# A bank for q's maxima, a three-part subtraction, integer weight assembly and a new step order, in a linear attention followed by two MLPs

## The chip, the cores and the metric

The kernel runs on one core of a Trainium2 chip. The metric is device time in microseconds (us) of one execution, lower is better. TensorE (PE) multiplies matrices, VectorE (DVE) and ScalarE (ACT) do elementwise work, GpSimd (POOL) does a little of it, and SyncE (SP) issues nearly all DMAs.

## The reference, cut to what matters

```python
def phi(x):                                   # q, k: (4, 8, 576, 64)
    proj = einsum('bhsd,df->bhsf', x, w_phi)  # w_phi: (64, 128)
    proj = proj - max(abs(proj), axis=-1, keepdims=True)
    return concatenate([exp(proj), exp(-proj)], axis=-1)
q_p, k_p = phi(q), phi(k)
kv = einsum('bhsf,bhsd->bhfd', k_p, v);  z = sum(k_p, axis=2)
x = einsum('bhsf,bhfd->bhsd', q_p, kv) / (einsum('bhsf,bhf->bhs', q_p, z)[..., None] + 1e-6)
x = x.transpose(0, 2, 1, 3).reshape(2304, 512)
h = ((x @ w1) * (x @ w2)) @ w3                # w1, w2: (512, 1024), w3: (1024, 1024)
x = h @ w_out                                 # (1024, 512)
r = maximum(x @ w_in, 0.0)                    # (512, 2048)
out = (r * r) @ w_out2                        # (2048, 512)
```

The MLP weights arrive as 64-bit floats, which the kernel reads as pairs of 32-bit words and turns into 32-bit floats itself.

## The kernel before

**Attention.** The work is 16 pairs of heads (4 batches, 4 pairs each). A pair has 512 tokens and a tail of 64; the tails of two pairs share tiles. For each pair named steps are run; the order in which the engines get them is written out by hand: `START` for the first slots, then `SLOT` for even and `ODD` for odd slots, then `END`, which lets attention run into the first products of the MLP. In slot t most steps serve pair t; `turn_k`, `turn_q` and their `high`/`low` parts already serve pair t+1, `out`, `keep`, `keep_values`, `reciprocals` and `quotients` serve pair t-1, `turn_x` and `keep_x` pair t-2. Each engine executes its own instructions in the order of the list.

**The steps of q.** `project_q` and `project_qt` multiply q and its tail by w_phi into the PSUM tiles `pq[0]` (two banks) and `pq[1]` (one bank, of which 128 of 512 columns are used). There is one such set, so a pair's projection waits until `exp_q1` and `exp_qt` of the pair before have read it. `max_q` and `max_qt` (DVE, L455) take maxima over blocks of 32, `max_rows` (PE, L463) transposes them into `pm`, `max_parts` (DVE, L468 to L471) takes the rest of the maximum and splits it into a high and a low part, `send` (SP, L477) copies the two by two small DMAs into the tile `mrow`, and `minus_q` (PE, L485) subtracts them from `pq` with three matmuls against a tile of -1. `exp_q0`, `exp_q1` and `exp_qt` (ACT, L492 and L499) follow.

**The other steps.** `project_k`, `peak_k`, `less_k`, `exp_k` do the same for k, whose maximum needs no transposing; `values` multiplies exp(k) by v (L513), `out` multiplies exp(q) by that (L545, L553) into the PSUM tile `po`, `keep` (ACT, L561) copies `po` out, `reciprocals` and `quotients` (DVE, POOL) divide, `turn_x` (PE) transposes the result into `po` again and `keep_x` copies it out. Before the change `pm` is a part of `po`, so `out` has to wait until `max_parts` has read it.

**Weights.** There are 72 blocks of 128x512 weights: 18 are decoded beside attention (the list `beside`; the steps `w-1`, `w0`, `w1` advance them, some seven advances a block and about one block a slot), 54 during the MLPs. `decoding` loads a block (`w-1`), scales the high word on ACT (L149), shifts it and puts the sign in on DVE (L151, L154), isolates the exponent and scales the low word by it on DVE (L158, L161), and adds the two as floats on POOL or, for the second MLP, on DVE (L166). Then the weight is split into a rounded part (ACT) and a rest (POOL or DVE).

Of the kernel before, what the change touches and what calls it, by code (L numbers as in the profile page):

```python
# [31 lines left out]
project_k0/0 low_tail/-1 project_qt/0 max_q/0 max_qt/0 peak_k0/0 fetch_q/0 project_k2/0 less_k0/0 exp_k0/0 max_rows/0  # L32
max_parts/0 project_k1/0 send/0 w-1/0 turn_k/0 high_k/0 peak_k1/0 less_k1/0 warm2/0 w0/0 peak_k2/0 exp_k1/0 less_k2/0
store_x/0 w0/0 low_k/0 warm4/0 turn_q/0 minus_q/0 high_q/0 w0/0 values0/0 values1/0 keep_values/0 exp_q0/0
fetch_tails/0 out/0 project_k1/1 exp_k2/0 keep/0 fetch_q/1 tail_values/0 load_v/0 store_x/1 exp_q1/0 exp_qt/0 low_q/0
project_q/1 keep_values/1 project_qt/1 project_k0/1 w0/0 fetch_k/1 turn_k/1 max_q/1 max_qt/1 w0/1 w-1/1 peak_k0/1 w1/1
max_rows/1 max_parts/1 high_k/1 w1/1 less_k0/1 send/1 low_k/1 peak_k1/1 less_k1/1 exp_k0/1 out/1 turn_q/1 keep/1
exp_k1/1 turn_tails/1 high_q/1 reciprocals/1 quotients/1 minus_q/1 exp_q0/1 w0/1 values0/1 exp_q1/1 exp_qt/1 low_q/1
w0/1 fetch_q/2 keep_tails/1 w0/1 values1/1 low_tail/1 project_k0/2 w0/2 tail_values/1 fetch_k/2 project_q/2
keep_values/2 project_qt/2 turn_x/2 keep_x/2 max_q/2 max_qt/2 project_k1/2 turn_k/2 max_rows/2 peak_k0/2 less_k0/2  # L40
# [17 lines left out]
fetch_k/13 project_q/13 fetch_q/13 project_qt/13 tail_values/12 turn_x/13 w0/13 keep_values/13 keep_x/13 project_k0/13
max_q/13 max_qt/13 turn_k/13 w1/13 w1/13 max_rows/13 peak_k0/13 less_k0/13 max_parts/13 exp_k0/13 send/13 w-1/13
project_k1/13 store_x/13 out/13 high_k/13 keep/13 peak_k1/13 less_k1/13 turn_q/13 low_k/13 turn_tails/13 exp_k1/13  # L60
reciprocals/13 quotients/13 high_q/13 minus_q/13 keep_tails/13 x_load/13 exp_q0/13 values0/13 w0/13 low_tail/13
exp_q1/13 exp_qt/13 w0/13 values1/13 low_q/13 w0/13 load_v/13 tail_values/13 keep_values/14 project_q/14 project_qt/14
turn_x/14 keep_x/14 project_k1/14 max_q/14 max_qt/14 project_k0/14 w1/14 w0/14 peak_k0/14 turn_k/14 less_k0/14
high_k/14 max_rows/14 max_parts/14 send/14 w-1/14 w1/14 exp_k0/14 out/14 peak_k1/14 keep/14 less_k1/14 exp_k1/14
reciprocals/14 quotients/14 low_k/14 turn_q/14 project_k2/14 peak_k2/14 minus_q/14 values0/14 less_k2/14 high_q/14
exp_q0/14 low_q/14 w0/14 w0/14 exp_q1/14 exp_qt/14 values1/14 exp_k2/14 project_q/15 project_qt/15 tail_values/14
turn_x/15 late/15 max_q/15 max_qt/15 w0/14 keep_values/15 keep_x/15 w1/15 w1/15 project_k0/15 peak_k0/15 w0/15
project_k1/15 less_k0/15 max_rows/15 max_parts/15 peak_k1/15 x_split0/15 x_split1/15 exp_k0/15 out/15 send/15
store_x/15 x_split2/15 product_a0/15 keep/15 minus_q/15 reciprocals/15 quotients/15 less_k1/15 w0/15 exp_k1/15
exp_q0/15 w-1/15 values0/15 x_split3/15 values1/15 turn_w3/15 product_a1/15 w0/15 keep_a/15 split_w3/15 w0/15  # L70
tail_values/15 prefetch/15 product_b/16 exp_q1/15 exp_qt/15 keep_values/16 w1/17 turn_w3b/16 turn_x/16 keep_x/16 w1/16
# [1403 lines left out]
```

## Time and profile before

| | |
|---|---|
| runs of this kernel | 918.45, 919.26, 919.79 us; median 919.26 |
| the profiled execution | 918.55 us, of which the span from first to last instruction is 916.8 us |
| PE busy | 886.7 us (97% of the span) |
| DVE, ACT, POOL busy | 646.0, 382.4, 112.5 us |
| granted TensorE clock | 0.999 of full |
| attention | about the first 200 us, the MLPs the rest |

The profile is of one execution. Busy times are sums over the span; a group's mean is the length of one instruction, and the lengths of pipelined instructions overlap, so starts are the better measure of what one costs its engine.

### The profile page before, as it was taken

To read this page: it belongs to the slowest core of one execution; us is meant where nothing else is said; L and a number is where in the kernel's file an instruction comes from. 1 tells how busy PE (TensorE), PEld (TensorE's weight loads), DVE (VectorE), ACT (ScalarE), POOL (GpSimd) and SP (SyncE) were. 2 spreads that over 40 slices of the span, in tenths; PEclk is the share of its full clock that TensorE was granted. 3 is DMA by queue.
4 is the path that set the end of the run, shared out by engine and by line. 5 is a ranking of instruction groups with operands and counts; after the bars stand their busy time and mean duration, and the time that the engine had idled before them with its cause. 6 is when DMAs were issued, how large, how long until landed. Compare 5 with 4: busy or idle time off the path is not lost.

```text
span 916.8 us, 16526 instructions
## 1 busy us (share of the span) xinstructions
PE 886.7 (97%) x6468; PEld 775.1 (85%) x6468; DVE 646.0 (70%) x1215; ACT 382.4 (42%) x733; POOL 112.5 (12%) x112
## 2 busy tenths in 40 slices
PE   8889888899999999999999999999999999999998
PEld 6777777778888888998888889998889898989896
DVE  7877777778987788679999956566754447643533
ACT  5877777763434424454354422222421213321211
POOL 2333333322311450000000000000000000000000
PEclk9999999999999999999999999999999999999999
DMA  7456455547362436557898698597585655684621
GB/s 214 113 139 156 143 137 160 154 117 178 79 179 70 138 93 189 213 195 261 265 355 311 224 393 329 178 305 245 186 287 211 248 223 176 202 332 180 228 94 69
DMA packets 120653, 182.71 MB, mean 199 GB/s; under 512 B 60736, under 2 KB 80000, under 8 KB 120576
## 3 DMA queue, kind: packets, MB, share of 16 engines
q1 hardware_dynamic: 119520, 180.85, 59.9%
q8 instruction: 51, 0.84, 0.4%
q10 hardware_dynamic: 1056, 0.82, 0.3%
q14 instruction: 26, 0.21, 0.1%
HBM read 140.54 MB, written 40.89 MB: 198 GB/s over the span
## 4 chain that ended last, share of the span: by engine, by line
PE 86%; ACT 4%; DVE 4%; DMA 4%; issue 2%; SPq 0%; DVEq 0%
PE op L1321 21%; PE pa L252 11%; PE pb L252 10%; PE yp L1028 10%; PE ph_y L1285 8%; PE ph_x L1285 5%; PE ph_w L1285 5%; PE pf L955 5%; PE po L545 3%; DMA pair<-pair_hbm 2%; PE pq L440 2%; ACT kp L432 1%; PE pk L316 1%; DVE kmax L415 1%; ACT qp L492 1%
## 5 line engine op out<-in xcount | busy, mean ns | idle before, releaser
L1321 PE MATMUL op<-pair,r 128*128 128x512 f32 x864 | 202.9, 390 | 0.0
L1321 PEld LDWEIGHTS op<-pair,r 128*128 128x128 f32 x864 | 161.7, 188 | 32.2
L1028 PE MATMUL yp<-g,w3o 128*128 128x512 f32 (+1 forms) x480 | 105.1, 368 | 0.0
L1028 PEld LDWEIGHTS yp<-g,w3o 128*128 128x128 f32 x480 | 84.2, 189 | 15.0
L252 PE MATMUL pa<-c,w_w12a 128*128 128x512 f32 (+1 forms) x432 | 93.9, 366 | 0.0
L252 PE MATMUL pb<-c,w_w12b 128*128 128x512 f32 (+1 forms) x432 | 93.6, 365 | 0.0
L1285 PE MATMUL ph_y<-yf_t,pair 128*128 128x384 f32 x432 | 87.4, 336 | 0.1
L252 PEld LDWEIGHTS pa<-c,w_w12a 128*128 128x128 f32 x432 | 75.1, 189 | 13.7 <-DVE c L218 0.4
L252 PEld LDWEIGHTS pb<-c,w_w12b 128*128 128x128 f32 x432 | 75.2, 189 | 13.1
L1285 PEld LDWEIGHTS ph_y<-yf_t,pair 128*128 128x128 f32 x432 | 76.0, 188 | 1.5 <-DMA pair<-pair_hbm 0.7
L1372 DVE TENSOR_TENSOR u<-ph_y,m 128x384 f32<-128x384 f32 x24 | 13.4, 558 | 72.1 <-PE ph_y L1285 70.6
L1285 PE MATMUL ph_x<-yf_b,pair 128*128 128x384 f32 x288 | 58.4, 337 | 1.2 <-DMA pair<-pair_hbm 1.2
L1195 ACT ACTIVATE g<-g 128x512 fp32r<-128x512 f32 (+1 forms) x39 | 23.0, 589 | 81.8 <-DVE g L1193 81.8
L1285 PEld LDWEIGHTS ph_x<-yf_b,pair 128*128 128x128 f32 x288 | 51.2, 188 | 3.4 <-DMA pair<-pair_hbm 1.5
L1298 ACT ACTIVATE r<-m 128x384 fp32r<-128x384 f32 x43 | 22.6, 526 | 73.6 <-DVE m L1297 73.6
L432 ACT ACTIVATE kp<-kp 128x512 f32<-128x512 f32 (+1 forms) x80 | 47.2, 590 | 8.1 <-DVE kp L425 6.8
L545 PE MATMUL po<-kv,qp 128*64 128x65 f32 x1024 | 34.7, 223 | 11.9 <-DVE m L470 11.2
L545 PEld LDWEIGHTS po<-kv,qp 128*64 128x64 f32 x1024 | 31.8, 138 | 15.6 <-DVE m L470 14.7
L955 PE MATMUL pf<-w_wo,w3T 128*128 128x512 f32 x192 | 45.0, 390 | 0.0
L1368 ACT COPY m<-ph_x 128x384 f32<-128x384 f32 x24 | 11.5, 481 | 78.8 <-PE ph_x L1285 78.8
L955 PEld LDWEIGHTS pf<-w_wo,w3T 128*128 128x128 f32 x192 | 36.0, 188 | 7.5
L1299 DVE TENSOR_TENSOR r<-m,r 128x384 fp32r<-128x384 f32 x43 | 24.0, 559 | 25.4 <-ACT r L1298 25.4
(183 smaller groups left out, 1519.1 us busy)
## 6 DMA issues: line engine op xcount, KB each, us to landing
pair<-pair_hbm SPq DMA_DIRECT2D x144, 512.0 KB, 7.3
pair_hbm<-w_w SPq DMA_DIRECT2D x32, 512.0 KB, 6.0
raw_w<-in_moe_w_in_dram SPq DMA_DIRECT2D x16, 512.0 KB, 4.4
raw_w<-in_moe_w_out_dram SPq DMA_DIRECT2D x16, 512.0 KB, 4.6
pair_hbm<-v_w SPq DMA_DIRECT2D x16, 512.0 KB, 7.4
raw_w<-in_moe_w_dram SPq DMA_DIRECT2D x56, 128.0 KB, 3.3
x<-x_hbm SPq DMA_DIRECT2D x12, 512.0 KB, 6.3
yi<-y_hbm SPq DMA_DIRECT2D x12, 384.0 KB, 9.5
```

The costliest lines, as they stand in the source:

```text
L252: nc.tensor.matmul(ps[:, 0:n], a, c, start=kk + i == 0, stop=kk == KD - 1 and i == 2)
L432: nc.scalar.activation(z["kp", j][:, :, s, :], z["kp", j][:, :, 1, :], AF.Exp, scale=1.0 - 2.0 * s)
L440: nc.tensor.matmul(at[:, 0:width], wss[h, b, :], src[h, a, 0:width], start=n == 0, stop=n == 2)
L545: nc.tensor.matmul(po_t[half, j, i * E:(i + 1) * E], z["qp"][:, e, 2 * (i // 2) + j, at][:, half], z["kv"][:, e, j, :], start=i + e == 0, ...
L955: nc.tensor.matmul(pf, a, c, start=n == 0, stop=n == len(todo) - 1)
L1028: nc.tensor.matmul(blk.yp[i][:, 0:blk.n], a, d, start=c == blk.c0 and s == 0, stop=c == blk.c1 - 1 and s == 2)
L1195: nc.scalar.activation(g[:, 0, 0:n], g32[:, 0:n], AF.Copy)
L1285: nc.tensor.matmul(ps_, a, c, start=start and n == 0, stop=n == 5, skip_group_check=not start)
L1298: nc.scalar.activation(r[:, 0], h, AF.Copy)
L1299: nc.vector.tensor_tensor(out=r[:, 1], in0=h, in1=r[:, 0].bitcast(F32), op=ALU.subtract)
L1321: nc.tensor.matmul(z.ops[i], a, d, start=z.p + j + s == 0, stop=z.p == NP2 - 1 and j == 1 and s == 2)
L1372: nc.vector.tensor_tensor(out=u2, in0=y, in1=m1, op=ALU.add)
```

## The change

`pm` moves from `po` into the free columns of `pq[1]`. `mrow` shrinks from 128x1536 to 128x512: the maxima of the three 512-column parts lie in three pairs of rows (0 and 1, 32 and 33, 64 and 65), and each of the three matmuls of `minus_q` contracts over its own two rows, in its own 32-row group of the array, instead of over 128 rows that are mostly zero. The memset of `mrow` goes. In `decoding` the two DVE instructions that isolate the exponent and scale the low word give way to one instruction, on POOL for the 18 blocks beside attention and on ACT for the other 54, and the addition becomes one of integers. `START`, `SLOT`, `ODD` and `END` get a new order of the same steps.

```diff
 SLOT = """
-fetch_q fetch_k project_q project_qt turn_x keep_values keep_x project_k0 max_q max_qt project_k1 w1 w1 w0 turn_k
-peak_k0 max_rows high_k less_k0 max_parts send fetch_tails w-1 store_x exp_k0 out peak_k1 less_k1 keep turn_q low_k
-project_k2 exp_k1 reciprocals quotients peak_k2 less_k2 high_q minus_q exp_q0 values0 low_q w0 w0 exp_q1 exp_qt exp_k2
-w0 values1 load_v
+fetch_q w0 turn_x keep_values project_q max_q project_qt fetch_k project_k0 max_qt w1 project_k1 w1 keep_x fetch_tails
+turn_k peak_k0 w-1 store_x high_k less_k0 exp_k0 max_rows out turn_q peak_k1 project_k2 values0 keep max_parts less_k1
+low_k high_q exp_k1 reciprocals send minus_q quotients values1 peak_k2 exp_q0 w0 w0 exp_q1 exp_qt w0 less_k2 low_q
+exp_k2 load_v
 """.split()
 ODD = """
-fetch_q fetch_k project_q project_qt tail_values< turn_x keep_values keep_x project_k0 max_q max_qt project_k1 w1 w1
-w0 turn_k peak_k0 max_rows high_k less_k0 max_parts send w-1 store_x exp_k0 out peak_k1 less_k1 keep turn_q low_k
-turn_tails exp_k1 reciprocals quotients high_q minus_q keep_tails exp_q0 values0 low_q w0 w0 exp_q1 exp_qt w0 values1
-low_tail load_v tail_values
+fetch_q project_k0 project_q project_qt fetch_k tail_values< max_q keep_values turn_x turn_k max_qt peak_k0 keep_x w1
+max_rows less_k0 w1 project_k1 w0 out high_k w-1 peak_k1 turn_q max_parts exp_k0 less_k1 store_x turn_tails keep low_k
+exp_k1 high_q reciprocals values0 send keep_tails minus_q w0 quotients exp_q0 tail_values w0 exp_q1 values1 low_q
+low_tail exp_qt load_v w0
 """.split()
...
+    beside_attention = [True]
...
-        e, w = y, t.bitcast(F32)
+        w = t.bitcast(F32)
         nc.scalar.activation(y.bitcast(F32), hi.bitcast(F32), AF.Copy, scale=2.0 ** -112)
         yield
-        nc.vector.tensor_scalar(
-            out=t, in0=y, scalar1=4, scalar2=1, op0=ALU.logical_shift_left, op1=ALU.logical_shift_right
-        )
+        nc.vector.tensor_scalar(out=t, in0=y, scalar1=3, scalar2=None, op0=ALU.logical_shift_left)
         nc.vector.scalar_tensor_tensor(
             out=t, in0=hi, scalar=-(1 << 31), in1=t, op0=ALU.bitwise_and, op1=ALU.bitwise_or
         )
         yield
-        nc.vector.tensor_scalar(
-            out=e, in0=t, scalar1=-(1 << 23), scalar2=None, op0=ALU.bitwise_and
-        )
-        nc.vector.scalar_tensor_tensor(
-            out=e.bitcast(F32), in0=lo.bitcast(mybir.dt.uint32), scalar=2.0 ** -52, in1=e.bitcast(F32),
-            op0=ALU.mult, op1=ALU.mult,
-        )
+        if beside_attention[0]:
+            nc.gpsimd.tensor_scalar(
+                out=y, in0=lo.bitcast(mybir.dt.uint32), scalar1=2.0 ** -29, scalar2=None, op0=ALU.mult
+            )
+        else:
+            nc.scalar.activation(y, lo.bitcast(mybir.dt.uint32), AF.Copy, scale=2.0 ** -29)
         yield
-        (nc.vector if name.startswith("w2") else nc.gpsimd).tensor_tensor(
-            out=w, in0=t.bitcast(F32), in1=e.bitcast(F32), op=ALU.add
-        )
+        (nc.vector if name.startswith("w2") else nc.gpsimd).tensor_tensor(out=t, in0=t, in1=y, op=ALU.add)
...
-        mrow = att.tile([P, NM * 32], F32R, bufs=1, name="mrow")
+        mrow = att.tile([P, 512], F32R, bufs=1, name="mrow")
...
-            z["pm"] = po_t[:, 0, 3 * P:4 * P]
-            nc.tensor.transpose(z["pm"], z["m1"], ident)
+            z["pm"] = pq[1][:, P:2 * P]
+            nc.tensor.matmul(
+                z["pm"], z["m1"], ident, is_transpose=True, start=False, stop=True, skip_group_check=True
+            )
...
-                    mrow[s:s + 1].bitcast(F32).rearrange("s (k r) -> s k r", r=32), z["mh"][:, s].bitcast(F32)
+                    mrow[s:s + 65:32].bitcast(F32).rearrange("i (k r) -> i k r", r=32), z["mh"][:, s].bitcast(F32)
...
-            for i, at, n in ((0, 0, C * P), (0, C * P, C * P), (1, 0, 2 * TAIL)):
-                row = i * 2 * C * P + at
+            for i, at in enumerate((pq[0][:, 0:C * P], pq[0][:, C * P:], pq[1][:, 0:2 * TAIL])):
+                two = slice(32 * i, 32 * i + 2)
                 nc.tensor.matmul(
-                    pq[i][:, at:at + n], minus, z["mrow"][:, row:row + n], start=False, stop=True, skip_group_check=True
+                    at, minus[two], z["mrow"][two, 0:at.shape[-1]], start=False, stop=True, skip_group_check=True
                 )
...
-        nc.vector.memset(mrow.bitcast(F32), 0.0)
...
+    beside_attention[0] = False
```

`START` and `END` are rearranged in the same manner (the first even slots and the last slots of attention with them).

## Rows read from the trace of the kernel before

**Rows 1.** Busy time of each engine in two stretches, one in attention, one in the MLPs
```profile
core 0: us, PE busy (x) PEld busy (x) DVE busy (x) ACT busy (x) POOL busy (x), PEclk, DMA share, GB/s
...
100.00:125.00 25.00, 22.26 (x381) 19.82 (x382) 19.23 (x39) 18.25 (x36) 8.68 (x9) 1.00 0.49 142
...
400.00:500.00 100.00, 100.00 (x465) 83.36 (x464) 93.81 (x186) 47.32 (x88) 0.00 (x0) 1.00 0.82 286
```
**Rows 2.** Waits of PE in the first 200 us: total, times, longest
```profile
PE po L545 <- DVE m L470: 11.2, 15, 1.3
PE pq L440 <- ACT qp L492: 6.1, 10, 0.8
```
**Rows 3.** Timeline of PE, slots 8 and 9: start, length, instruction, wait ahead
```profile
98.76 0.97 PE L440 MATMUL pq<-qT,wss 64*128 64x512 f32 x6 [0.69 <-ACT qp L492]
...
100.71 1.67 PE L316 MATMUL pk<-wbd,kT 128*128 128x256 f32 x12
...
102.65 0.27 PE L463 MATMUL po<-ident,m 128*128 128x128 f32 x1
103.56 1.15 PE L545 MATMUL po<-kv,qp 128*64 128x65 f32 x32 [0.64 <-DVE m L470]
...
107.36 0.76 PE L485 MATMUL pq<-mrow,minus 128*128 128x512 f32 x3 [0.30 <-DMA mrow<-mh]
108.04 2.09 PE L513 MATMUL pkv<-vs,kp 128*64 128x65 f32 x64
110.42 0.97 PE L440 MATMUL pq<-qT,wss 64*128 64x512 f32 x6 [0.29 <-ACT qp L492]
...
122.13 0.97 PE L440 MATMUL pq<-qT,wss 64*128 64x512 f32 x6 [0.69 <-ACT qp L492]
```
**Rows 4.** Timeline of DVE, slot 8
```profile
98.50 0.43 DVE L158 TENSOR_SCALAR dy_wo<-dt_wo 128x512 int32<-128x512 int32 x1
98.96 0.69 DVE L161 SCALAR_TENSOR_TENSOR dy_wo<-raw_wo,dy_wo 128x512 f32<-128x512 uint32 x1
...
99.91 1.44 DVE L455 TRANSPOSE_TENSOR_REDUCE m<-pq 128x32 f32<-128x1024 f32 x2
101.70 0.69 DVE L415 TENSOR_REDUCE kmax<-pk 128x4 f32<-128x512 f32 x1 [0.36 <-PE pk L316]
...
103.03 0.27 DVE L468 TENSOR_REDUCE mh<-po 48x32 fp32r<-48x128 f32 x1
...
103.54 0.18 DVE L471 TENSOR_TENSOR mh<-m,mh 48x32 fp32r<-48x32 f32 x1
```
**Rows 5.** Timeline of ACT, slot 8
```profile
106.16 0.70 ACT L561 COPY nd<-po 128x650 f32<-128x650 f32 x1 [1.53 <-PE po L553]
...
107.96 0.58 ACT L357 ACTIVATE qT<-pqt 128x512 fp32r<-128x512 f32 x1
108.44 1.93 ACT L492 ACTIVATE qp<-pq 128x1024 f32<-128x1024 f32 x2
```
**Rows 6.** The two DMAs of send in slots 8 and 9, issue to landing
```profile
L477 SPq DMA_DIRECT2D mrow<-mh x2: 557/564/572, 103.3 to 104.0; - x2
...
DMA to landing us min/median/max: 1.8/2.5/3.2
...
L477 SPq DMA_DIRECT2D mrow<-mh x2: 557/565/573, 115.3 to 116.0; - x2
...
DMA to landing us min/median/max: 1.8/1.8/1.8
```
**Rows 7.** Groups by shape in 30 to 185 us: total busy, mean ns of one
```profile
L166 POOL TENSOR_TENSOR dt_wo<-dt_wo,dy_wo 128x512 f32<-128x512 f32 x7 | 8.9, 1273 | 16.3 <-DVE dy_wo L161 16.3
...
L149 ACT ACTIVATE dy_wo<-raw_wo 128x512 f32<-128x512 f32 x5 | 3.4, 683 | 0.0
```
**Rows 8.** Timelines of POOL and DVE, the same moment in the MLPs
```profile
219.47 1.40 POOL L166 TENSOR_TENSOR dt_w<-dt_w,dy_w 128x512 f32<-128x512 f32 x1 [6.53 <-DVE dy_w L161]
...
219.76 1.66 DVE L161 SCALAR_TENSOR_TENSOR dy_w12a<-raw_w12a,dy_w12a 128x512 f32<-128x512 uint32 x1
```
**Rows 9.** The page's part on DMA queues: packets, MB, share of 16 engines' span
```profile
q1 hardware_dynamic: 119520, 180.85, 59.9%
```

More of the change, by code (lines that the diff above doesn't have):

```diff
@@ L31 @@
 warm6/0 fetch_k/0 turn_q/-1 turn_k/-1 high_q/-1 low_q/-1 high_k/-1 project_q/0 turn_tails/-1 keep_tails/-1 low_k/-1
[L32 to L40, printed above, removed]
@@ L41 @@
-w1/2 high_k/2 max_parts/2 out/2 exp_k0/2 peak_k1/2 fetch_tails/2 send/2 keep/2 load_v/1 less_k1/2 w1/2 turn_q/2 w0/2
-project_k2/2 low_k/2 reciprocals/2 quotients/2 peak_k2/2 exp_k1/2 less_k2/2 minus_q/2 high_q/2 values0/2 store_x/2
-exp_q0/2 exp_q1/2 exp_qt/2 w0/2 w-1/2 w0/2 values1/2 low_q/2 load_v/2 exp_k2/2
+project_k0/0 low_tail/-1 project_qt/0 max_qt/0 max_q/0 peak_k0/0 project_k2/0 less_k0/0 exp_k0/0 project_k1/0
+max_rows/0 max_parts/0 send/0 w-1/0 turn_k/0 fetch_q/0 high_k/0 peak_k1/0 store_x/0 less_k1/0 warm2/0 w0/0 peak_k2/0
@@ new lines @@
+exp_k1/0 less_k2/0 w0/0 low_k/0 warm4/0 turn_q/0 minus_q/0 high_q/0 fetch_q/1 w0/0 values0/0 values1/0 fetch_tails/0
+exp_k2/0 keep/0 keep_values/0 out/0 tail_values/0 exp_q0/0 project_k1/1 load_v/0 store_x/1 exp_q1/0 exp_qt/0 low_q/0
+project_q/1 keep_values/1 project_qt/1 fetch_k/1 project_k0/1 w0/0 w0/1 turn_k/1 max_q/1 high_k/1 max_qt/1 peak_k0/1
+w1/1 w-1/1 max_rows/1 max_parts/1 w1/1 less_k0/1 send/1 peak_k1/1 low_k/1 exp_k0/1 out/1 less_k1/1 turn_q/1 keep/1
+exp_k1/1 turn_tails/1 reciprocals/1 high_q/1 quotients/1 minus_q/1 exp_q0/1 w0/1 values0/1 exp_q1/1 exp_qt/1
@@ new lines @@
+keep_tails/1 low_q/1 w0/1 w0/1 values1/1 low_tail/1 tail_values/1 project_k0/2 fetch_q/2 w0/2 fetch_k/2 keep_values/2
+project_q/2 project_qt/2 turn_x/2 keep_x/2 max_q/2 max_qt/2 project_k1/2 max_rows/2 peak_k0/2 less_k0/2 turn_k/2
+max_parts/2 high_k/2 out/2 w1/2 exp_k0/2 peak_k1/2 keep/2 fetch_tails/2 send/2 load_v/1 less_k1/2 low_k/2 w1/2
+turn_q/2 w0/2 project_k2/2 reciprocals/2 exp_k1/2 quotients/2 peak_k2/2 less_k2/2 minus_q/2 high_q/2 values0/2
+exp_q0/2 store_x/2 exp_q1/2 exp_qt/2 low_q/2 w0/2 values1/2 w-1/2 w0/2 load_v/2 exp_k2/2
@@ L56 @@
+low_tail exp_qt load_v w0
 """.split()
 END = """
[L58 to L71, printed above, removed]
@@ L72 @@
-early/16 split_w3b/16 w0/17 w0/16 out/16 w0/16 gate/16 keep/16 w-1/16 prefetch/17 reciprocals/16 quotients/16 last/16
-w1/17 w1/16 w0/16 w0/17 w0/17 w0/16 w0/17 prefetch/16
+fetch_q/13 fetch_k/13 project_q/13 project_qt/13 turn_x/13 tail_values/12 w1/13 project_k0/13 w0/13 keep_values/13
+keep_x/13 max_q/13 max_qt/13 turn_k/13 max_rows/13 peak_k0/13 less_k0/13 w1/13 max_parts/13 exp_k0/13 send/13
+project_k1/13 store_x/13 out/13 w-1/13 high_k/13 keep/13 peak_k1/13 less_k1/13 turn_q/13 low_k/13 exp_k1/13
@@ new lines @@
+turn_tails/13 high_q/13 reciprocals/13 quotients/13 minus_q/13 keep_tails/13 x_load/13 exp_q0/13 values0/13 w0/13
+low_tail/13 exp_q1/13 exp_qt/13 w0/13 values1/13 low_q/13 w0/13 load_v/13 tail_values/13 project_k0/14 project_q/14
+keep_values/14 project_qt/14 turn_x/14 keep_x/14 project_k1/14 max_q/14 max_qt/14 w1/14 peak_k0/14 less_k0/14
+turn_k/14 high_k/14 w0/14 max_rows/14 max_parts/14 send/14 peak_k1/14 w-1/14 w1/14 out/14 exp_k0/14 keep/14 less_k1/14
+exp_k1/14 reciprocals/14 quotients/14 turn_q/14 low_k/14 project_k2/14 peak_k2/14 minus_q/14 values0/14 high_q/14
@@ new lines @@
+exp_q0/14 low_q/14 exp_q1/14 w0/14 less_k2/14 w0/14 exp_qt/14 values1/14 exp_k2/14 turn_x/15 project_q/15
+project_qt/15 tail_values/14 late/15 max_q/15 max_qt/15 w0/14 keep_x/15 w1/15 w1/15 project_k0/15 peak_k0/15 w0/15
+keep_values/15 project_k1/15 max_rows/15 less_k0/15 store_x/15 max_parts/15 peak_k1/15 x_split0/15 x_split1/15
+exp_k0/15 out/15 x_split2/15 send/15 product_a0/15 keep/15 minus_q/15 reciprocals/15 quotients/15 less_k1/15 w0/15
+exp_k1/15 exp_q0/15 values0/15 values1/15 x_split3/15 turn_w3/15 w0/15 product_a1/15 w-1/15 keep_a/15 exp_qt/15
@@ L74 @@
+split_w3/15 w0/15 tail_values/15 prefetch/15 w0/17 product_b/16 keep_values/16 w1/17 exp_q1/15 turn_x/16 turn_w3b/16
+keep_x/16 w1/16 early/16 out/16 w0/16 gate/16 keep/16 reciprocals/16 prefetch/17 split_w3b/16 w-1/16 quotients/16
+w0/16 last/16 w1/17 w1/16 w0/16 w0/17 w0/17 w0/16 w0/17 prefetch/16
 """.split()
@@ L157, in decoding @@
         yield
-        nc.vector.tensor_scalar(
-            out=e, in0=t, scalar1=-(1 << 23), scalar2=None, op0=ALU.bitwise_and
-        )
-        nc.vector.scalar_tensor_tensor(
-            out=e.bitcast(F32), in0=lo.bitcast(mybir.dt.uint32), scalar=2.0 ** -52, in1=e.bitcast(F32),
-            op0=ALU.mult, op1=ALU.mult,
-        )
+        if beside_attention[0]:
[4 more added lines that the diff above has]
+            nc.scalar.activation(y, lo.bitcast(mybir.dt.uint32), AF.Copy, scale=2.0 ** -29)
         yield
-        (nc.vector if name.startswith("w2") else nc.gpsimd).tensor_tensor(
-            out=w, in0=t.bitcast(F32), in1=e.bitcast(F32), op=ALU.add
-        )
+        (nc.vector if name.startswith("w2") else nc.gpsimd).tensor_tensor(out=t, in0=t, in1=y, op=ALU.add)
         got.append(w)
-        spare[name] = e.bitcast(F32)
+        spare[name] = y.bitcast(F32)
     def decode_splitting(src, name, got, tile_of=unit):
```

## The prediction

> **What bounds the kernel now.** I read the busy times by stretch first, then PE's waits, then the timelines of two neighbouring slots on every engine. The stretches split the kernel: in the MLPs PE is busy for all of its 100 us, in attention for 22.26 of 25 us [rows 1]. So nothing that DVE, ACT or POOL gain in the MLPs can shorten them, and what the change can win lies in the first 200 us. There PE's largest waits are 11.2 us in 15 pieces, `out` waiting for `max_parts` over the shared bank, and 6.1 us in 10 pieces, `project_q` waiting for the exponentials [rows 2].
>
> Summing PE's waits would be the wrong reading, because the slots are a loop. `pq` exists once, so projection follows projection: 98.76, 110.42, 122.13 [rows 3], or 11.66 and 11.71 us a slot. Follow the loop in slot 8. `project_q` starts at 98.76; the maxima run on DVE from 99.91 for 1.44 us; PE is at `max_rows` only at 102.65, behind the k projections; `max_parts` runs on DVE from 103.03 to 103.72 [rows 3, 4]. The second DMA is issued at 104.0 and needs 3.2 us [rows 6], so `minus_q` starts at 107.36, after a wait of 0.30 us for it [rows 3]. ACT is still at qT until 108.44, then does the two exponentials in 1.93 us [rows 5], and the next projection starts. So `out`'s wait of 0.64 us is not a link of this loop by itself: it delays `keep` on ACT (106.16), which stands in front of the exponentials, and in a slot where the DMA lands late that costs nothing. In slot 9 the DMAs land in 1.8 us [rows 6]; there the ACT side is the later one. Six of the 16 slots (0, 2, 4, 6, 8, 10) show a landing above 3.0 us, as slot 8; the other ten read like slot 9.
>
> **The change part by part.** Times in the next two paragraphs are counted from the start of `project_q`, with start-to-start costs from [rows 3 to 5]: projection and its tail 1.17 us, two k projections 1.50, `turn_k` 0.44, k's maximum and its subtraction 0.65 to 0.7 each, `out`, `turn_q` and the third k projection together 3.5 (103.56 to 107.06), half of `values` 1.0, `max_parts` 0.69.
>
> *Even slot, new order.* `turn_x` now stands ahead of `project_q`, under the exponentials' tail, so PE reaches `max_rows` at 3.1 instead of 3.89. But DVE does `peak_k0`, `less_k0` and `peak_k1` first, so `max_parts` runs from 4.6 to 5.3 instead of 4.27 to 4.96. The second DMA goes out at 5.55 and lands at 7.35 (with 1.8 us) or 8.75 (3.2). PE does `out` from 3.4 with no wait, and `values0` before `minus_q`, and is free at 7.9. `minus_q` thus starts at 7.9 or 8.8. ACT, whose `keep` now starts at about 5.95 instead of 7.40, is through `high_q` and `exp_k1` at 8.3. `minus_q`'s length is bounded between the present 0.76 us and 0.49: side by side the three matmuls take one stream of 512 columns instead of 1152, and six matmuls in two 64-row groups already take only 0.97 us [rows 3], so I take 0.49. The exponentials end at 10.35 or 11.25: that is the slot, against 11.66.
>
> *Odd slot.* `project_k0` goes ahead of `project_q`, and `max_parts` again ends near 5.3. ACT has one step more before the exponentials and is ready at 8.45, so the slot takes 10.35 with a landing of 1.8 us and 11.15 with one of 3.2, against 11.71.
>
> A pair of slots falls from 23.37 to 20.7 or 22.4 us: 1.3 or 0.5 us a slot. With the ten short and six long landings of the present trace, 1.0 us a slot; over the 14 slots from the second projection to the last, 14.0 us.
>
> *DVE's two instructions* per weight block, 0.43 and 0.69 us [rows 4], 1.12 us in all, leave DVE between `low_q` and `max_q`. They end just as the projection does, so they cost the loop little now and I count no gain of their own; without them DVE is merely early. In the MLPs their going wins nothing, since PE covers it.
>
> *POOL's new instruction* in attention is not in the trace. Below it is bounded by nothing, above by the two-input form at 1.27 us [rows 7]; I take 1.27. POOL is busy for 8.68 of 25 us [rows 1], and the block that it finishes is needed by ACT about 2.5 us into the next slot, so it is hidden up to a length of some 2.5 us. A POOL instruction can hold a DVE one with two SBUF inputs: such a one took 1.66 us beside a POOL instruction, and 0.69 elsewhere [rows 4, 8]. In the loop only L471 is of that kind, 0.18 us long; the new order puts POOL's work either after the slot's `quotients` or some 2 us ahead of L471. I count nothing, at most 0.97 us a slot.
>
> *ACT's new instruction*, 54 times in the MLPs, is priced by the scaling of the high word, 0.68 us [rows 7]; 37 us in all on an engine that is busy for 47 of 100 us [rows 1]. I count nothing: PE has two or more products of 12 matmuls between what ACT copies out and where it is used. If that cover were gone, it would cost up to 0.68 us a block.
>
> *Queues.* `w-1`, `store_x` and, in slots 2, 6 and 10, the four DMAs of `fetch_tails` now stand in front of `send` on SP. A DMA costs SP about 0.6 us to issue (two in 1.2, [rows 6]). Only the tails reach `send`: four issues and a weight load put it back by some 0.6 us in three slots, 1.8 us. The memset of `mrow` lies under the arrival of the first inputs: nothing. `START` and `END` I leave at nothing, within 3 us either way.
>
> *The shape of the two DMAs.* The destination goes from 48 pieces on one partition to 16 pieces on each of three. The mean packet occupies an engine for 0.599 x 16 x 916.8 / 119520 = 0.073 us [rows 9]. If the 48 pieces went through three engines, 16 packets each, the transfer would take 16 x 0.073 = 1.2 us where three packets take 0.2: up to 1.0 us more, which hits the odd slots for about 0.4 us (the even ones wait for PE), some 3 us in all. I count nothing in the likeliest case and keep 3 for the range. The Trainium skill speaks for the longer one: DMA: Bandwidth & Descriptors, section on why a DMA increments its semaphore by 16, has a copy spread over the largest number of engines up to 16 that divides the slowest dimension of both sides, here 3 and 48 where it was 48 and 48. By that rule the time would be some 3 us above my forecast; no row shows on how many engines a copy runs.
>
> The sum: 918.55 - 14.0 + 1.8 = 906.35 in the measure of the profiled execution (1.75 us of it outside the span). It lies 0.7 us under the median of the three runs, so 907 us to be compared with 919.26.
>
> **The rivals.**
> 1. *PE becomes the bound.* If landing and ACT are quicker than I laid them out, a slot is PE's own work: 22.26/25 of 11.69 us is 10.4 [rows 1, 3], less 0.27 for `minus_q`, 10.1. That saves 1.55 x 14 = 22 us: 897. For it speaks that the new order gives PE something to do at each place where it waited; against it, `max_parts` is later on DVE than it was.
> 2. *The landing decides everywhere.* All landings at 3.2 us, or three engines for each of the two DMAs besides: 0.5 us a slot at best, 7 us less the 1.8 and up to 3, so 912 to 917. For it: the weight load now precedes `send`, and the large loads and stores share the engines with it.
> 3. *Slower: ACT stalls the MLPs.* The new ACT instruction waits for DVE to have read the tile that it overwrites, and the copy of a product out of PSUM stands behind it. With 0.68 us for each of 54 blocks on PE's path, 37 us come on top: up to 944. It decides from 0.23 us a block (12.2/54). Against it: PE is full in these stretches [rows 1], with DVE near full beside it, and DVE loses 1.12 us a block.
> 4. *No change.* The loop is held by ACT's in-order steps at the present pace, and the gain is spent on the tails and on rival 3 in small: 918 to 920.
>
> **How the numbers follow.** My forecast, 902 to 912, gets 0.55; PE's own bound 0.16; landings everywhere 0.14; no change 0.07; slower 0.08. The likeliest time is 907. Leaving out the far end of the first rival and the last two, the range is 897 to 917. What a measurement of this kernel can tell from no change is about 0.2%, or 1.8 us: faster 0.85, same 0.07, slower 0.08.
>
> **What would show it.** In the profile after, PE's wait on `max_parts` at `out` must be gone; successive projections should lie 10.3 to 11.2 us apart, and the interval should follow the landing of the second DMA; `minus_q`'s three matmuls should take about 0.5 us; the MLPs should still show PE at 100% and be as long as before, from the end of attention on. I am wrong if projections lie 11.5 us apart or more, if PE has new waits on ACT after 200 us, or if POOL's new instruction takes above 2.5 us and ACT waits for it in attention.

## The result, and the profile after

The changed kernel takes 905.84 us (median of four runs, 905.21 to 906.49) against 919.52 (four runs too, one more than in the table above): a ratio of 0.985 (95% interval 0.9835 to 0.9869), 13.7 us faster. The forecast was 907. Of the two profiled executions the spans are 916.8 and 904.4 us, 12.4 us apart; the forecast's sum was 12.2.

Where the 12.4 us came from, by the starts of four things in both traces:

| stretch | before | after | gained |
|---|---|---|---|
| up to the second projection | 18.88 | 18.33 | 0.55 |
| second projection to the last (14 slots) | 162.19 | 154.04 | 8.15 |
| last projection to the first product of w_out with w3 (L955, now L953) | 21.05 | 19.42 | 1.63 |
| the rest, to the end | 714.6 | 712.6 | 2.0 |

The loop of slots, from which I had expected 12.2, gave 8.15; the ends and the MLPs, which I had left at nothing, gave the other 4.2. So the total came out right partly by luck: two misses cancel, and the experiments had to say why.

PE's waits of the first 200 us come first, as in [rows 2]: total, times, longest.

```profile
PE pq L483 <- DMA mrow<-mh: 7.0, 9, 2.6
PE pk L312 <- DVE kp L421: 1.7, 4, 0.5
...
PE pq L436 <- ACT qp L490: 1.0, 1, 1.0
```

`out`'s wait for `max_parts` (11.2 us) is gone, and the wait of `project_q` for the exponentials has shrunk from 6.1 to 1.0. In their place PE waits for the copied maxima, once for 2.6 us. The timeline of PE, slots 8 and 9, answers [rows 3]:

```profile
95.42 0.97 PE L436 MATMUL pq<-qT,wss 64*128 64x512 f32 x6
...
98.74 1.15 PE L543 MATMUL po<-kv,qp 128*64 128x65 f32 x32
...
103.25 0.50 PE L483 MATMUL pq<-mrow,minus 2*128 2x512 f32 x3
...
105.33 0.92 PE L312 MATMUL pk<-wbd,kT 128*128 128x256 f32 x6 [0.49 <-DVE kp L421]
106.18 0.96 PE L436 MATMUL pq<-qT,wss 64*128 64x512 f32 x6
...
115.58 0.50 PE L483 MATMUL pq<-mrow,minus 2*128 2x512 f32 x3 [1.68 <-DMA mrow<-mh]
...
118.12 0.96 PE L436 MATMUL pq<-qT,wss 64*128 64x512 f32 x6
```

Slot 8 lasts 10.76 us; `minus_q` starts 7.83 us into it (forecast 7.9), waits for nothing, and its three matmuls take 0.50 us (0.49). Slot 9 lasts 11.94, because `minus_q` waits 1.68 us. All 14 intervals between projections: 10.03, 10.28, **14.41**, 10.77, 10.41, 10.77, 10.42, 10.76, **11.94**, 10.78, 10.76, 10.38, **11.83**, 10.50 (before: 10.39 to 12.01, most of them 11.65 to 11.70). The DMA queue of SP shows what slots 3 and 9 have in common (start, issue time; slot 5, without a wait, stands between them for comparison):

```profile
41.65 0.41 SPq L143 DMA_DIRECT2D raw_wo<-in_moe_w_out_dram  x1
42.16 0.38 SPq L608 DMA_DIRECT2D x_hbm<-xm  x1
43.37 1.94 SPq L475 DMA_DIRECT2D mrow<-mh  x2
...
64.37 0.41 SPq L143 DMA_DIRECT2D raw_wo<-in_moe_w_out_dram  x1
67.00 0.34 SPq L608 DMA_DIRECT2D x_hbm<-xm  x1
68.55 1.64 SPq L475 DMA_DIRECT2D mrow<-mh  x2
...
108.38 0.42 SPq L143 DMA_DIRECT2D raw_w12a<-in_moe_w_dram  x1
109.36 0.34 SPq L608 DMA_DIRECT2D x_hbm<-xm  x1
110.91 1.65 SPq L475 DMA_DIRECT2D mrow<-mh  x2
```

In both, a weight load and a store, 512 KB each, go out just ahead of the two small copies. The same pair stands ahead of them in slots 5, 7 and 11 too, but there the load went out 3.3 to 4.2 us before the first copy, against 1.7 and 2.5 us in slots 3 and 9, and the wait is nothing or, in slot 11, 0.49 us. In slots 6 and 10 a weight load (behind the tails' small ones) goes out 0.8 and 0.65 us before it, without a store, and the wait is at most 0.19 us. Slot 13 has neither ahead of its copies and waits 0.54 us; what makes it 11.83 us long no run here asks. In slot 3 the wait costs more than its 2.63 us. The busy times by stretch show it: in 46 to 49 us PE has next to nothing to do, then the granted clock (the third number from the right) falls:

```profile
46.00:49.00 3.00, 0.36 (x15) 0.23 (x11) 1.94 (x4) 1.17 (x3) 2.92 (x3) 1.00 0.72 246
49.00:52.00 3.00, 3.00 (x41) 2.67 (x43) 0.00 (x0) 2.38 (x5) 1.38 (x2) 0.54 0.00 0
52.00:56.00 4.00, 4.00 (x36) 3.51 (x33) 1.86 (x3) 1.81 (x4) 1.27 (x1) 0.92 0.45 128
60.00:100.00 40.00, 38.73 (x691) 33.96 (x691) 31.29 (x62) 33.41 (x67) 23.51 (x20) 1.00 0.58 168
...
400.00:500.00 100.00, 100.00 (x448) 83.05 (x447) 78.46 (x155) 58.01 (x107) 0.00 (x0) 1.00 0.78 279
```

The mean of 0.54 in 49 to 52 us means that nearly all of that stretch ran at the lower of the two levels, 1.2 of 2.4 GHz. In slots without such a wait PE is now busy for 38.73 of 40 us; before it was 22.26 of 25 [rows 1]. In the MLPs PE is full as before, DVE has fallen from 93.81 to 78.46 us in 100 and ACT risen from 47.32 to 58.01.

The new instructions beside attention (30 to 185 us: total busy, mean ns), to be set against [rows 7]:

```profile
L158 POOL TENSOR_SCALAR dy_wo<-raw_wo 128x512 int32<-128x512 uint32 x6 | 9.8, 1641 | 0.5
L164 POOL TENSOR_TENSOR dt_wo<-dt_wo,dy_wo 128x512 int32<-128x512 int32 x6 | 7.7, 1278 | 0.5
...
L153 DVE SCALAR_TENSOR_TENSOR dt_wo<-raw_wo,dt_wo 128x512 int32<-128x512 int32 x6 | 5.8, 970 | 0.2
L158 POOL TENSOR_SCALAR dy_w12a<-raw_w12a 128x512 int32<-128x512 uint32 x3 | 5.5, 1848 | 0.3
...
L152 DVE TENSOR_SCALAR dt_wo<-dy_wo 128x512 int32<-128x512 int32 x6 | 3.5, 576 | 0.0
```

POOL's instruction is longer than the 1.27 us that I took. DVE's two remaining instructions have stretched: the same two took 418 and 692 ns before, so a block costs DVE 1.55 us where four instructions took 2.23, and the 1.12 us that went give 0.7 net. The new instruction is not the reason; the new order is, which puts POOL's `quotients` (L578) beside them. First slot 8 of this kernel, then slot 8 of the run old_order below, which has POOL's new instruction but the order of before:

```profile
102.72 1.58 POOL L578 TENSOR_TENSOR xd<-nd,rc 128x320 f32<-128x320 f32 x2 [3.80 <-DVE rc L569]
102.92 0.80 DVE L152 TENSOR_SCALAR dt_w12a<-dy_w12a 128x512 int32<-128x512 int32 x1
103.75 1.09 DVE L153 SCALAR_TENSOR_TENSOR dt_w12a<-raw_w12a,dt_w12a 128x512 int32<-128x512 int32 x1
```

```profile
101.93 0.42 DVE L152 TENSOR_SCALAR dt_w12a<-dy_w12a 128x512 int32<-128x512 int32 x1
102.38 0.69 DVE L153 SCALAR_TENSOR_TENSOR dt_w12a<-raw_w12a,dt_w12a 128x512 int32<-128x512 int32 x1
102.44 2.02 POOL L158 TENSOR_SCALAR dy_w12a<-raw_w12a 128x512 int32<-128x512 uint32 x1 [0.75 <-DVE dt_w12a L152]
```

In old_order the means of the first group are 418 and 692 ns again, and in old_decode and behind_lo_act, which have the new order and no such POOL instruction in attention, they are 575 to 577 and 969 to 970.

And the part on DMA queues, against [rows 9]:

```profile
q1 hardware_dynamic: 119104, 180.84, 60.0%
```

There are 416 packets fewer, 13 for each of the 32 copies; each run with the new copy has 119104 packets and each with the old copy 119520. That is what 3 engines in place of 16 make if each of them adds one packet to a copy; no view shows the single engines. The Trainium skill (DMA: Bandwidth & Descriptors, the section on why a DMA increments its semaphore by 16) has 3 engines here, each ending its share with a write to the semaphore, and the count agrees.

### The profile page after: what moved, and what is told of

Its sections match the earlier page's. It is cut to its first block, busy times and chain, and to the rows that moved or that the text cites. A ratio compares the mean times of both kernels' runs of the same rounds, so it can differ in the third digit from the quotient of the medians.

```text
span 904.4 us, 16486 instructions
## 1 busy us (share of the span) xinstructions
PE 886.6 (98%) x6468; PEld 773.7 (86%) x6468; DVE 568.5 (63%) x1070; ACT 412.2 (46%) x787; POOL 147.8 (16%) x130
## 3 DMA queue, kind: packets, MB, share of 16 engines
q1 hardware_dynamic: 119104, 180.84, 60.0%
## 4 chain that ended last, share of the span: by engine, by line
PE 89%; DVE 4%; ACT 3%; DMA 2%; issue 1%; POOL 0%; SPq 0%; DVEq 0%; POOLq 0%
PE op L1319 22%; PE pa L248 11%; PE pb L248 11%; PE yp L1026 11%; PE ph_y L1283 8%; PE ph_x L1283 6%; PE ph_w L1283 6%; PE pf L953 5%; PE pk L312 2%; PE pq L436 2%; DMA mrow<-mh 2%; PE po L543 2%; PE pkv L511 2%; PE pkv L521 1%; PE po L584 1%
## 5 line engine op out<-in xcount | busy, mean ns | idle before, releaser
L1191 DVE TENSOR_TENSOR g<-pb,a 128x512 f32<-128x512 f32 (+1 forms) x39 | 24.8, 636 | 51.9 <-PE pb L248 51.7
L1366 ACT COPY m<-ph_x 128x384 f32<-128x384 f32 x24 | 11.5, 480 | 74.2 <-PE ph_x L1283 74.2
L953 PE MATMUL pf<-w_wo,w3T 128*128 128x512 f32 x192 | 44.9, 390 | 0.0
L451 DVE TRANSPOSE_TENSOR_REDUCE m<-pq 128x4 f32<-128x128 f32 (+1 forms) x32 | 23.2, 762 | 33.9 <-PE pq L436 25.2
L953 PEld LDWEIGHTS pf<-w_wo,w3T 128*128 128x128 f32 x192 | 36.0, 188 | 7.5
```

Of the source, the lines that this page charges most:

```text
L451: nc.vector.tensor_reduce(z["m1"][:, at // 32:(at + n) // 32], pq[i][:, 0:n].rearrange("p (n r) -> p n r", r=32), AX.X, ALU.max, apply_abs ...
L953: nc.tensor.matmul(pf, a, c, start=n == 0, stop=n == len(todo) - 1)
L1191: nc.vector.tensor_tensor(out=g32[:, 0:n], in0=pb[:, 0:n], in1=a_sb[:, 0:n], op=ALU.mult)
```

## The experiments

**Theory.** The slot loop around the single `pq` gains about 1.0 us; two slots lose much of it because large transfers stand ahead of `send`; bank, order and subtraction give the loop's gain together, decoding nothing. **Rivals.** PE's waits simply add up (the bank alone gives most); the copy is late because it runs on three engines; decoding on DVE matters. Each run also has the time of the kernel before on the same chip, 917.8 to 918.1.

### First round: one part alone, or one part undone

**bank_alone**: the kernel before, with `pm` in the free columns of `pq[1]` and nothing else.

```diff
-            z["pm"] = po_t[:, 0, 3 * P:4 * P]
-            nc.tensor.transpose(z["pm"], z["m1"], ident)
+            z["pm"] = pq[1][:, P:2 * P]
+            nc.tensor.matmul(z["pm"], z["m1"], ident, is_transpose=True, start=False, stop=True, skip_group_check=True)
```

> The kernel before with one edit: the transposed maxima go to the free columns of q's second PSUM tile, everything else as before. Loop theory: out's wait of 0.64 us is a link of the loop only in the ten slots where the copies of the maxima land in 1.8 us, so 3 to 6 us are won, 913 to 916 us. Rival, PE's waits add up: the 11.2 us go, about 908. Rival, DVE's relief made the gain: nothing, 918 to 920.

Measured 909.91 us, ratio 0.9902 (0.9885 to 0.9919): 8.0 us from three lines, more than the loop as I had followed it allowed. From slot 3 on the intervals are 10.90 to 11.36 instead of about 11.7. The rival, that the waits add up, was nearer with its 908: `out`'s wait was a link of the loop in nearly every slot, by way of `keep` and ACT's order. ACT's timeline of slot 8, whose projection starts at 98.05, shows it beside [rows 5]:

```profile
104.73 0.70 ACT L563 COPY nd<-po 128x650 f32<-128x650 f32 x1 [0.82 <-PE po L555]
...
107.01 1.93 ACT L494 ACTIVATE qp<-pq 128x1024 f32<-128x1024 f32 x2
```

Counted from the projection, `keep` starts at 6.68 us (7.40 before) and the exponentials at 8.96 (9.68 before): both 0.7 us earlier, as the slot is shorter.

**old_order**: the changed kernel with the four lists `START`, `SLOT`, `ODD` and `END` of before.

> The changed kernel with the four step lists of the kernel before; bank, subtraction and weight decoding as changed. Loop theory: the three edits alone win 4 to 7 us of the 13.7, 912 to 915 us, the rest is the order's. Rivals (waits add up, or DVE's relief): as the changed kernel, 905 to 908.

Measured 902.80, ratio 0.9829 (0.9814 to 0.9843): 3 us *faster* than the changed kernel (2 us by the ratios), outside what either side expected. The new order, as it stands, is a part that costs; the intervals of the two ratios overlap a little, but old_decode_mlp below, with the changed kernel's attention, lies clear of this run (0.9847 to 0.988). PE's waits of this run, first 200 us:

```profile
PE pq L436 <- ACT qp L490: 5.7, 11, 0.9
PE pq L483 <- DMA mrow<-mh: 5.6, 10, 0.8
```

In the old order, with everything else new, ACT holds `project_q` as before, but no wait for the copy exceeds 0.8 us, and from slot 3 to slot 12 the intervals alternate between 11.0 and 10.6 without an exception.

**old_decode**: the changed kernel with the decoding of before, in attention and MLPs.

> The changed kernel with the old weight decoding everywhere (two DVE instructions more a block, no POOL or ACT instruction more). Loop theory: DVE's two instructions now stand in front of the low part of the next q and cost up to 0.5 us in even slots, 906 to 910 us, and the MLPs stay as long. Rival, DVE's relief made the gain: 913 or more.

Measured 914.20 (ten runs, 909.9 to 917.9), ratio 0.9961 (0.9941 to 0.998): 8.4 us lost where I had counted nothing. The runs go with the granted clock: 909.90 us at a mean of 0.998, 917.93 at 0.988. The chain that ended last, in slot 8 of this run (start, length, what):

```profile
104.42 0.88 DVE dt_w12a L152
105.32 1.10 DVE dt_w12a L155
...
106.52 0.44 DVE dy_w12a L159
106.98 0.69 DVE dy_w12a L162
107.67 0.34 DVE kp L426
...
108.15 1.62 PE pk L317 x6
```

All four instructions of a block stand between k's maximum and its subtraction on DVE, and PE waits behind them with the k projection that the new order put ahead of `project_q` (four such waits, 7.0 us in all).

**old_minus**: the changed kernel with `mrow`, `send` and `minus_q` of before (one partition a row, contraction over 128 rows).

> The changed kernel with the old layout of the maxima's rows: one partition per part as destination of the two copies, three matmuls over 128 rows. If the copies land late because they run on three engines instead of 16, PE's wait for them falls from 7.0 us to under 3 and that pays for 0.27 us more in each subtraction: 903 to 907 us. Rival, the landing does not depend on the shape and the loads issued just ahead of the copies delay them: the waits stay, and the longer subtraction costs 2 to 4 us, 908 to 910.

Measured 915.83 (ten runs), ratio 0.9976 (0.9965 to 0.9987): 10 us lost, more than any theory had. PE's wait for the copy rose to 12.1 us, the longest 3.6; in slot 3 the two copies, on sixteen engines, took 5.4 and 5.8 us from issue to landing. Its runs, too, go with the granted clock (914.4 us at 0.998, 918.3 at 0.994). Three engines are not what makes the copy late.

### Second round: the loads behind send, and the subtraction by itself

**behind**: in `SLOT` and `ODD` the loads and the store are issued directly after `send`.

```diff
-... w1 keep_x fetch_tails turn_k peak_k0 w-1 store_x high_k ... reciprocals send minus_q ...
+... w1 keep_x turn_k peak_k0 high_k ... reciprocals send fetch_tails w-1 store_x minus_q ...
-... high_k w-1 peak_k1 ... less_k1 store_x turn_tails ... values0 send keep_tails ...
+... high_k peak_k1 ... less_k1 turn_tails ... values0 send w-1 store_x keep_tails ...
```

> The changed kernel with the weight load, the store of x and the tails' loads issued directly behind send instead of ahead of it, in the even and the odd slots. Theory: it is the two 512 KB transfers ahead of send that make the copy of the maxima land late. In the changed kernel the two slots with both of them ahead of send last 14.41 and 11.94 us, the undisturbed ones 10.4 and 10.77. Then PE's waits of 2.63 and 1.68 us at minus_q go, the slots become 10.4 to 10.8 throughout, and the kernel takes 905.8 - 3.6 - 1.2 = 901 us, 899.5 to 902.5. Rival, the copy is late because it runs on three engines: the transfers stay in the same rings and only change places, waits of 1.5 us or more remain in some slots, 904 to 907.

Measured 902.13, ratio 0.9826 (0.9811 to 0.984). The two long slots are gone: slots 3 and 9 last 10.41 and 10.42 us (slot 13 stays long, 12.16), and the granted clock stays at 1.00 in 30 to 60 us, where it was 0.94. From the second projection to the last it takes 148.88 us, 13.3 less than before; the forecast had 14.0 ahead of its deduction for queues. PE's busy time in the middle slots, same columns as above:

```profile
60.00:100.00 40.00, 39.12 (x699) 34.38 (x697) 30.56 (x63) 32.34 (x66) 20.97 (x19) 1.00 0.58 158
```

Against old_order the new order, with its loads behind, gains 0.7 us, and the intervals overlap: a gain from the order in the whole kernel is not shown. The traces show one in `END`: from the last projection to the first product of w_out with w3 every kernel with the new order takes 19.4 us, every one with the old order and the new bank 20.4.

**behind_oldminus**: behind, with the old subtraction and copy.

> The kernel of the run behind (loads and store directly behind send), with the maxima sent to one partition a row and subtracted by matmuls that contract over 128 rows, as before. Theory: minus_q's start-to-end grows by 0.26 us a slot and the copy of the maxima to one partition lands no later than to three: 14 slots by 0.26, some 4 us more than the run behind, 904 to 907. Rival A, sixteen engines in place of three: the copy lands 1 us sooner where it is awaited, and the time is within 2 us of the run behind. Rival B, the old layout has a cost of its own beside these (it took 915.8 us with the loads ahead of send, 10 us above the changed kernel): 910 or more, with waits above 2 us at minus_q.

Measured 904.86, ratio 0.9858 (0.9843 to 0.9872); its runs (904.28 to 905.79) lie all above those of behind (900.90 to 902.97). The size is near the theory's, its reason is not: the middle slots last 10.48 to 10.88 us, nearly as in behind (10.41 to 11.02) but for one of 11.52. From the second projection to the last 2.9 us are lost, about half of them in slot 1 (11.42 against 10.05, with a wait of 1.30 us for the copy).

**bank_minus**: the kernel before, with the bank and the three-part subtraction; old decoding, old order.

> The kernel before, with the maxima's bank and the three two-row matmuls (and their copy to three partitions), but the old decoding and the old order. Theory: with the bank alone it is 909.9 us and its slots are 10.94 to 10.99; minus_q is 0.26 us shorter, which the loop through the exponentials gives back in each slot: 14 by 0.26 = 3.6 us, so 906.3, 905 to 908; the decoding is then worth the remaining 3 to 4 us to the 902.8 of the old order with everything else new. Rival, DVE's two instructions cost nothing in the old order: 902 to 904, and the three-row subtraction gives 7 us. Rival 2, a copy on three engines lands 1 us later: 909 to 914.

Measured 906.58, ratio 0.9872 (0.9857 to 0.9886). Again the expected sum, and again not from its source: the middle slots are 10.94 to 11.00 us, as with the bank alone. The difference lies in the first two, 12.37 and 10.29 us against 14.07 and 13.43. Matmul or copy? The third round asks. Against old_order, the decoding is worth 3.8 us in the old order (2.0 between the two profiled executions).

**old_decode_mlp**: the changed kernel with the old decoding in the MLPs only.

> The changed kernel with the old decoding in the MLPs' 54 blocks only; attention as changed. Theory: PE is busy for all of the MLPs either way, so neither DVE's relief nor ACT's new instruction shows there: 905 to 907, the length from the first product to the end within 1 us of the changed kernel's 712.6. Rival: the 2 us that the MLPs are shorter than before come from DVE's relief: 907 to 909, with a PE wait of about 1 us after 200 us. Rival 2: the ACT instruction costs the MLPs something: 902 to 904.5.

Measured 905.74, ratio 0.9863 (0.9847 to 0.988), the changed kernel's time. All of the 8.4 us of decoding lies in attention; neither DVE's relief nor ACT's 54 instructions show in the MLPs. The 2 us by which the profiled MLPs were shorter are thus not shown to be the change's: over all profiled runs that stretch took 712.5 to 713.4 us with the new decoding there and 712.7 to 714.6 with the old, ranges that overlap.

### Third round: what is in the subtraction and the decoding

**bank_copy**: bank_minus, but its matmuls contract over 128 rows, each against a weight tile of its own. Only the copy is new beside bank_alone.

```diff
+        minus3 = att.tile([P, 3, P], F32R, bufs=1, name="minus3")
+        nc.vector.memset(minus3.bitcast(F32), 0.0)
+        for i in range(3):
+            nc.vector.memset(minus3[32 * i:32 * i + 2, i].bitcast(F32), -1.0)
+        nc.vector.memset(mrow.bitcast(F32), 0.0)
...
-                    at, minus[two], z["mrow"][two, 0:at.shape[-1]], start=False, ...
+                    at, minus3[:, i], z["mrow"][:, 0:at.shape[-1]], start=False, ...
```

> The kernel of the run bank_minus (old order, old decoding, new bank, maxima copied to three partitions), but the three matmuls of minus_q contract over all 128 rows, each against a weight tile of its own that is -1 in the two rows of its part and 0 elsewhere. Two theories of the 3.3 us between bank_alone (909.9) and bank_minus (906.6), whose middle slots last the same 10.94 to 11.00 us. Theory, the copy: on three partitions it lands sooner while the first loads run (bank_alone waits 1.85 and 1.96 us in the first two slots, bank_minus 0.78 and 0.50), so the matmul's shape is worth nothing and this run takes 906.5, 905.5 to 907.5, its first two intervals about 12.4 and 10.4. Rival, the matmul's shape: 0.26 us in each of 14 slots come back, 909 to 911, with intervals of 11.2.

Measured 906.65, ratio 0.9877 (0.986 to 0.9893), as bank_minus, with `minus_q` at 0.76 us. So the matmul's shape is worth nothing, and the copy's shape 3.3 us; the runs (906.44 to 907.19) lie all below those of bank_alone (909.07 to 911.67). The added memsets cost this run about 0.9 us at the start (PE waits 2.0 us for the tile `minus` instead of 1.1). Without the start, from the second projection to the last, it is 155.84 us in bank_alone, 151.82 here and 151.68 in bank_minus. PE's timeline, slots 1 and 2, first bank_alone, then bank_copy:

```profile
19.60 0.97 PE L440 MATMUL pq<-qT,wss 64*128 64x512 f32 x6
27.29 0.76 PE L487 MATMUL pq<-mrow,minus 128*128 128x512 f32 x3 [1.96 <-DMA mrow<-mh]
33.03 0.97 PE L440 MATMUL pq<-qT,wss 64*128 64x512 f32 x6
```

```profile
19.39 0.96 PE L440 MATMUL pq<-qT,wss 64*128 64x512 f32 x6
25.65 0.76 PE L486 MATMUL pq<-mrow,minus 128*128 128x512 f32 x3 [0.53 <-DMA mrow<-mh]
29.85 0.96 PE L440 MATMUL pq<-qT,wss 64*128 64x512 f32 x6
```

In bank_alone the second copy, issued at 23.6, lands 3.6 us later. In bank_copy the two issues end at 24.33, and `minus_q` starts at 25.65. The rest of slot 1 is the clock once more: in bank_alone it is 0.74 and 0.77 in the stretches after the wait (27 to 34 us).

**behind_old_decode**: behind, with the old decoding beside attention.

> The kernel of the run behind (902.1) with the old decoding beside attention; the MLPs decode as changed. Theory: in the new order DVE's two instructions, 0.44 and 0.69 us, stand ahead of the last part of less_k, for which PE waits with project_k0, in the odd slots (one block a slot, half of the slots hit), so 1.1 us in 7 of 14 slots, 8 us: 910, 908 to 912, the odd-slot intervals at 11.9 to 12.7. Rival: the 8.4 us that the old decoding cost in the changed kernel came by way of the loads ahead of send, which are gone here: 902 to 905, as the 3.8 us it is worth in the old order at most.

Measured 910.21 (908.33 to 913.25), ratio 0.992 (0.9895 to 0.9945): the theory's 910. The loss is the same with the loads out of the way, so they are not its cause. PE waits for `less_k` four times, 7.0 us in all and 1.8 at the longest, and slots 4 to 10 last 11.81 to 12.98 us. Even and odd ones are long, not the odd ones alone; the clock is at 0.93 in 50 to 100 us. The two runs at a mean clock of 0.998 took 908.33 and 908.45 us, those at 0.993 and 0.989 took 911.98 and 913.25: some 6 us of the loss come without a lower clock, up to 5 more with one.

**behind_lo_act**: behind, with the low word's instruction on ACT in attention too.

> The kernel of the run behind (902.1) with the new instruction on the low word on ACT in attention too, 0.67 us there in place of 1.55 to 1.85 us on POOL. Theory: POOL is off the path (a third to a half busy), ACT is on it in every second slot, so 0.67 us for each of 15 to 18 blocks shows in about half of the slots: 5 us, 905 to 909. Rival, POOL's instruction holds DVE's (its two-input form takes 0.98 to 1.09 us in attention beside POOL and 0.69 elsewhere) and that is on the path: 899 to 901.5. Between them, 901.5 to 905, neither is on the path.

Measured 905.67, ratio 0.9869 (0.9855 to 0.9884): 3.5 us slower. PE's wait for the exponentials rises from 0.9 us (once) to 5.2 (seven times). So 0.67 us on ACT is on the path where 1.55 to 1.85 on POOL are hidden.

**behind_less**: behind, with `less_k2` ahead of the weight steps in the even slots.

```diff
-... values1 peak_k2 exp_q0 w0 w0 exp_q1 exp_qt w0 less_k2 low_q exp_k2 load_v
+... values1 peak_k2 less_k2 exp_q0 w0 w0 exp_q1 exp_qt w0 low_q exp_k2 load_v
```

> The kernel of the run behind (902.1) with less_k2 moved ahead of the three weight steps in the even slots, so that DVE's shift and sign (0.80 and 1.09 us) no longer stand between k's maximum and its subtraction, for which PE waits 0.5 us with project_k0 four times. Theory: these waits go, 7 slots by up to 0.3 to 0.5 us: 899 to 901. Rival: PE is busy for 39.12 of 40 us in the middle of that run, so nothing more than 0.2 us a slot is there, and what waits is only moved: 901.5 to 903, the same.

Measured 900.66 (899.44 to 901.37, five runs), ratio 0.9808 (0.9794 to 0.9821). It is the fastest kernel of this study, 5 us below the changed one. PE's wait for `less_k` is gone; the step from behind is 1.5 us, but the two intervals overlap, so that step is likely and not established.

## Why the prediction was right, and which of its steps were not

Put together by runs in the old order, the bank gives 8.0 us, the shape of the copy 3.3, the shape of the matmul nothing and the decoding 3.8: 918 to 902.8 us. The new order, as it stands, gives 3 back (2 by the ratios to before): 905.8. That the total came out (12.4 us between the profiled executions, 12.2 forecast) is luck as to its terms: the loop gained 4 us less than its 12.2, the rest 4 us more than nothing.

- **The slot.** A pair of undisturbed slots takes 10.76 + 10.41 = 21.2 us (forecast 20.7 to 22.4). The 1.0 us a slot was right, and with the loads moved the loop gains 13.3 us of the 14.0. Three of the 14 intervals are above the 11.5 us that I had named as a sign of being wrong. What sets an undisturbed slot is not what I had named, the landing or ACT: there `minus_q` starts without a wait, and in 200 us `project_q` waits for the exponentials once. PE is busy for 97% of the slot, rival 1's mechanism, at 10.6 us a slot instead of the 10.1 that I had worked out, and most of the rest (0.98 of 1.27 us in 60 to 100 us) is a wait for DVE's `less_k`.
- **Queues: failed.** "Only the tails reach `send`", 1.8 us in three slots. The slots with the tails' loads ahead of `send` are not longer than others; two odd slots with a weight load and a store at most 2.5 us ahead of it are, by 4.0 and 1.5 us over the 10.41 of their kind. I had looked at the issue time on SP (0.6 us each in the forecast) and not at the data. That what stands ahead delays the copy is shown by behind; that it is 1 MB still being moved fits the slots in which the load went out earlier and nothing waited.
- **The copy's shape: wrong sign.** I kept +3 us for three engines; it gives 3. The number of engines was as the Trainium skill has it, as far as the packets tell, but the transfer was no longer for it. On sixteen engines it lands in 1.8 us at best; on three its landing is not in the trace, but where PE waits for it with nothing in front, `minus_q` starts 2.0 to 2.1 us after the second copy's issue begins (1.9 after one on sixteen). In slot 1 that was 2.1 us on three engines (23.6 to 25.65) where the copy on sixteen took 3.6 to land. In the old order no wait for the copy on three engines ended more than 2.2 us after that issue began; on sixteen, in the kernel before and in bank_alone, waits ended up to 3.9 us after it. That a copy over sixteen engines waits for the fullest of them fits this; no view shows the single engines, so it is argued only. SP's issue of a copy rose from 0.56 to some 0.78 us, which no slot was seen to feel.
- **The bank: right, under-valued.** I had written of `out`'s wait that "in a slot where the DMA lands late that costs nothing"; without that wait nearly all slots are 0.7 us shorter, slot 8 too, whose landing I had called late.
- **The subtraction.** 0.50 us as taken (0.49), and worth nothing in the old order, where the 0.26 us goes into ACT's order, which holds `project_q` (5.8 us of waits in bank_minus). In the new order the matmuls were not changed alone; most middle slots of behind_oldminus are at most 0.1 us longer than those of behind.
- **Decoding: failed.** "I count no gain of their own; without them DVE is merely early." It is worth 3.8 us in the old order and 6 to 8 in the new one, because there the weight steps stand ahead of `less_k2`, and PE's next k projection now goes ahead of `project_q`. I had followed DVE only from `low_q` to `max_q`.
- **POOL and ACT: right.** POOL's instruction took 1.5 to 2.0 us, above my bound of 1.27 but below the 2.5 that it may last. It is hidden: PE waits for POOL nowhere, ACT for its sum three times, 1.6 us in all. The 0.4 us more that DVE's two instructions take in a block are not its price but that of `quotients` beside them, and so of the new order; I had looked for such a hold at L471 alone. Rival 3 (ACT stalls the MLPs) is out: PE has no wait after 200 us.
- **START and END.** They lie inside the 3 us that I had left open: 0.55 and 1.63 us gained, of the latter 0.7 with the bank and 0.95 with the new order.

## What to carry to other kernels

Follow every engine around the loop, not only the chain that is longest now: when one link goes, the order on DVE or ACT behind it becomes the next, and two weight instructions in the wrong place cost 6 to 8 us, about what the shared bank gave. Before moving a load ahead of a small copy that someone awaits, count the bytes that it puts in front, not the issue time. And undo each part on its own: the fastest kernel here uses all the parts but not the order as it came, and the old order with all other parts takes some 2 us more than it, with intervals that overlap.
